# A planned attention and expert kernel: fixing the order of the program on TensorE alone

## Chip, cores and metric

The kernel runs on one core of a Trainium2 chip. The metric is the device time of one execution in microseconds (us). The time before is 265.57 us, the median of three runs (264.77 to 265.9).

The engines are named as in the profile: PE is TensorE (PEld its weight loads), DVE is VectorE, ACT is ScalarE, POOL is GpSimd, and SP only issues DMAs. L143 is line 143 of the kernel.

## What is computed

The input `x` has 2048 tokens of 512 features, in bf16. The result is a sum of three parts:

```
xn  = layernorm(x)
out = x + A(xn) + B(xn)

A: 32 heads of 16 features, the tokens in 4 segments of 512; per segment s
     a_dot = softmax(q k^T / 4 + causal mask) v       within the segment
     a_mem = phi(q) M / (phi(q) z)                     M, z: sums over earlier segments
     o     = g * a_mem + (1 - g) * a_dot
     M    += phi(k)^T v ;  z += sum phi(k)             phi(t) = t + 1 if t > 0, else exp(t)
   A = o @ wo

B: r = xn @ w_r ; the one token with the largest r gets
     (silu(x_sel @ w_gate) * (x_sel @ w_up)) @ w_down * sigmoid(r), added to its row of xn
```

## The kernel before

**Tiles and stages.** Tokens lie in 16 blocks of 128 (`NB`). The attention is walked in 160 steps (`NT`, loop at L735), 40 for each segment. Five steps make a unit of four heads. Each step does three things: `score` (L446) lets PE multiply keys and queries into one of two PSUM tiles `st`; `exp` (L456) lets ACT take the exponential of 128 x 1024 values into `pt` and POOL put zeros above the diagonal (L465); and `pv` (L468) lets PE multiply `pt` with the values into `acc`. In the loop, step t does the exponential of t, the scores of t + 2 and the values product of t - 2 (`LAG = 2`). After each unit DVE divides by the sums (`evac`, L482).

**Fillers.** All other work is written as small generator functions, and at the end of each step `fill` (L646) puts pieces of them between the steps. Each has an earliest step, a due step and a cost in ns of PE's time; `fill` emits so much of them, the most urgent first, that all are done by their due steps. A "pause" in such a function lets some steps pass, so that what it has asked of another engine may be done before PE goes on. The fillers that matter here:

- `g_ln` (L253) does the layer norm of one group of four token blocks. `ln_stats` (L140) lets DVE run BATCH_NORM_STATS2 (L143) and BATCH_NORM_AGGREGATE (L144) on each of the four blocks of `x_all`, `ln_rstd` (L146) takes a logarithm and an exponential on ACT and computes `cvec` (L149) on DVE, `ln_xn` (L153) normalises the four blocks on POOL into the four buffers `xn` (L155), and `ln_T` (L157) transposes each on PE into PSUM, from where DVE copies it to `xnT` (L162). The first group is done in the same way ahead of the loop, with its `xn` on DVE.
- `g_projq`, `g_projk` and `g_projv` (L212, L232, L246) are the projections: PE multiplies into one of two PSUM tiles with the tag `misc`, and DVE moves the result to `raw_q`, `KT` or `Vaug`. SP scatters `raw_q` into `QZ` with eight DMAs.
- `phi_steps` (L191) computes phi with an exponential on ACT (`ex`), a minimum on POOL (`am`) and an addition and a maximum on DVE.
- `g_memT` (L379) transposes phi(k) on PE, and DVE copies it out (`pk`, L385). `g_mem` computes `a_mem` (`nm_ps`, `om`).
- `g_fin` transposes `Oseg`, multiplies with `wo`, adds the row of B and stores 128 tokens. `make_rb` (L490) computes what is added (`rb`, two buffers) on POOL.

**Loads.** SP issues the first four blocks of `x_all` and the weights `wq`, `wk` and `wv` first. ACT issues the other twelve blocks (L701, three DMAs of 512 KB) and `wo` (L702, 512 KB). They stand in the program behind the first group's projections. POOL issues three of the six loads of B's weights (`mw`, L125).

**What sets the order.** Each engine has its own list of instructions and works it in order; an instruction that waits holds up all behind it. A planner makes these lists at compile time. It knows which instruction needs which tile, counts time by its own table of costs, and puts instructions into an engine's list. Between L666 and L766 the program holds it to a rule: for each engine in a given set, the instructions, its DMA issues included, come in the order in which the program emits them. The order between engines, the engines that are not in the set, and the place of instructions from outside of this region stay the planner's. In the kernel before, the set holds PE, ACT, DVE and POOL, so only SP is left. The constants (L81 to L110) and SP's first loads are emitted ahead of the region. The branch for large logits (`slow_path`) comes behind it and isn't taken.

Of the kernel before, what the change touches and what calls it, by code (L numbers as in the profile page):

```python
# [14 lines left out]
ENG = mybir.EngineType  # L15
# [3 lines left out]
def build_kernel(ctx, tc, A_x, A_wq, A_wk, A_wv, A_wo, A_beta, B_x, B_w_r, B_w_gate, B_w_up, B_w_down, out, opts=None):  # L19
# [643 lines left out]
            pass  # L663


    manual = tc.manual_schedule(engines={ENG.PE, ENG.Activation, ENG.DVE, ENG.Pool})  # L666
    manual.__enter__()
    warm_ps = pst.tile([P, 2, L], f32, name="st", tag="st")
    for i in range(14):
# [172 lines left out]
@with_exitstack  # L842
def kernel(
    ctx: ExitStack,
    tc: tile.TileContext,
    A_x: bass.AP,
    A_wq: bass.AP,
    A_wk: bass.AP,
    A_wv: bass.AP,
    A_wo: bass.AP,  # L850
    A_beta: bass.AP,
    B_x: bass.AP,
    B_w_r: bass.AP,
    B_w_gate: bass.AP,
    B_w_up: bass.AP,
    B_w_down: bass.AP,
    out: bass.AP,
):
    build_kernel(ctx, tc, A_x, A_wq, A_wk, A_wv, A_wo, A_beta, B_x, B_w_r, B_w_gate, B_w_up, B_w_down, out)
# [34 lines left out]
```

## Time and profile before

| what | value |
|---|---|
| median of three runs | 265.57 us |
| the profiled execution's own time | 264.61 us |
| its span, from the first to the last instruction | 262.9 us |
| mean granted clock of PE | 0.948 |
| busy PE, ACT, DVE, POOL | 212.2, 177.0, 159.1, 155.0 us |

The span begins with the first instruction of the program and ends with the last; 1.7 us of the profiled execution lie around it. Busy time counts running instructions and not waits or DMA issues. In the lines of the profile, a bracket holds the idle time of the engine just before an instruction and what ended it. In the tables by window, each row has the stretch, its length, the busy us (and count) of PE, PEld, DVE, ACT and POOL, then PE's granted clock, the busy share of the DMA engines and GB/s. In a group's row, `x12 | 9.9, 836` is twelve instructions, 9.9 us together and 836 ns in the mean; behind the next bar is the idle time before them. In a row of the waits, `3.6, 6, 1.5` is us in total, times, and the longest.

### The profile page before, as it was taken

What the parts mean: (1) busy time and instruction counts of PE and PEld (TensorE: products, weight loads), DVE (VectorE), ACT (ScalarE), POOL (GpSimd) and SP (SyncE); (2) the same over time, 40 slices, a digit from 0 to 9 for tenths busy, and PEclk for the clock granted to TensorE, in tenths of its full rate; (3) what the DMA queues carried; (4) which work ended last, traced back from release to release, by engine and by line L of the source; (5) the groups of instructions that cost most, each with busy time, mean ns of one, the idle gap of its engine ahead of it and who ended that gap; (6) DMA issues with size and microseconds to landing.
All of it is one profiled execution on the core that took longest, in us unless ns stands there. A gap on an engine that the chain in (4) does not pass through costs nothing.

```text
span 262.9 us, 6843 instructions
## 1 busy us (share of the span) xinstructions
PE 212.2 (81%) x2677; PEld 138.5 (53%) x2717; DVE 159.1 (61%) x393; ACT 177.0 (67%) x202; POOL 155.0 (59%) x252
## 2 busy tenths in 40 slices
PE   8469977999786967789879888999888888988770
PEld 2224644656453734457555766665766455665530
DVE  6836395248764986355677686755647556565341
ACT  2124986989965968469577876969678587867600
POOL 9501459546629545749768846655568247967530
PEclk9767996899997999999999999999999799999997
DMA  6966510000000000000000004180001010101102
GB/s 187 304 248 185 158 27 16 10 14 13 14 10 10 13 10 6 7 5 18 13 11 10 15 2 143 24 287 17 16 24 29 14 42 21 61 25 40 44 6 87
DMA packets 14186, 14.38 MB, mean 55 GB/s; under 512 B 3184, under 2 KB 13616, under 8 KB 14144
## 3 DMA queue, kind: packets, MB, share of 16 engines
q1 hardware_dynamic: 11456, 9.00, 11.6%
q0 software_dynamic: 576, 2.75, 2.8%
q10 hardware_dynamic: 2112, 2.10, 2.6%
q8 instruction: 23, 0.38, 0.6%
q14 instruction: 19, 0.16, 0.2%
HBM read 9.71 MB, written 2.10 MB: 45 GB/s over the span
## 4 chain that ended last, share of the span: by engine, by line
PE 54%; DVE 26%; ACT 7%; POOL 7%; issue 4%; DMA 1%; DVEq 0%; ACTq 0%
PE st L453 19%; PE proj_ps L206 9%; PE acc L478 7%; ACT pt L458 7%; PE proj_ps L249 5%; POOL xn L155 4%; DVE bnst L143 4%; PE fin L514 4%; DVE om L420 2%; DVE KT L239 2%; DVE Oseg L487 2%; DVE ob L497 2%; DVE xn L155 1%; DVE raw_q L218 1%; POOL pt L465 1%
## 5 line engine op out<-in xcount | busy, mean ns | idle before, releaser
L458 ACT ACTIVATE pt<-st 128x1024 bf16<-128x1024 f32 x160 | 159.5, 1025 | 49.6 <-PE st L453 40.7
L465 POOL TENSOR_SCALAR_AFFINE_SELECT pt<-pt 128x512 bf16<-128x512 bf16 (+1 forms) x160 | 89.5, 567 | 74.0 <-ACT pt L458 72.3
L453 PE MATMUL st<-QZ,KT 128*128 128x256 bf16 (+3 forms) x502 | 96.5, 304 | 7.3 <-ACT pt L458 3.6
L478 PEld LDWEIGHTS <-pt 128*128 128x128 bf16 x1280 | 55.7, 97 | 32.5 <-POOL pt L465 8.3
L478 PE MATMUL acc<-Vaug,pt 128*128 128x17 bf16 x1280 | 56.3, 171 | 6.3 <-POOL pt L465 5.8
L453 PEld LDWEIGHTS <-KT 128*128 128x128 bf16 x512 | 42.4, 98 | 32.8 <-issue 12.4
L206 PE MATMUL proj_ps<-xnT,wk 128*128 128x512 bf16 x60 | 20.3, 408 | 2.4 <-DVE xnT L162 0.9
L485 DVE RECIPROCAL rr<-acc 128x16 f32<-128x16 f32 x32 | 8.2, 255 | 22.7 <-PE acc L478 22.5
L249 PE MATMUL proj_ps<-wv,xnT 128*128 128x512 bf16 x56 | 17.8, 409 | 2.0 <-DVE Vaug L251 0.6
L218 DVE CAST raw_q<-proj_ps 128x512 bf16<-128x512 f32 x15 | 10.4, 690 | 14.6 <-PE proj_ps L206 8.5
L427 POOL TENSOR_TENSOR Oseg<-Oseg,om 128x512 bf16<-128x512 bf16 x11 | 12.7, 1155 | 10.5 <-DVE cvec L149 4.0
L206 PE MATMUL proj_ps<-xnT,wq 128*128 128x512 bf16 x53 | 17.0, 397 | 2.1 <-DVE Vaug L251 1.2
L497 DVE SCALAR_TENSOR_TENSOR ob<-x_all,s,fin 128x512 bf16<-128x512 bf16 x14 | 10.3, 745 | 13.0 <-PE fin L514 10.6
L198 POOL TENSOR_SCALAR am<-ex 128x512 bf16<-128x512 bf16 x24 | 14.8, 617 | 4.5 <-DVE pkT L202 4.2
L251 DVE TENSOR_TENSOR Vaug<-proj_ps,omg_bc 128x512 bf16<-128x512 f32 x16 | 11.0, 690 | 10.0 <-PE proj_ps L249 8.2
L239 DVE CAST KT<-proj_ps 128x512 bf16<-128x512 f32 x15 | 10.3, 684 | 11.3 <-PE proj_ps L206 9.7
L487 DVE TENSOR_TENSOR Oseg<-acc,rr 128x256 bf16<-128x256 f32 x32 | 13.6, 425 | 1.1
L492 POOL TENSOR_SCALAR rb<-ybc,onehot,cvec 128x512 bf16<-128x512 bf16 x16 | 12.6, 793 | 2.2 <-DVE ybc L374 2.2
L155 POOL TENSOR_SCALAR xn<-x_all,rstd,cvec 128x512 bf16<-128x512 bf16 x12 | 9.9, 836 | 5.1 <-DVE cvec L149 5.1
L514 PE MATMUL fin<-wo,oT 128*128 128x512 bf16 x42 | 12.1, 378 | 0.3
L143 DVE BATCH_NORM_STATS2 bnst<-x_all 128x6 f32<-128x512 bf16 x16 | 10.7, 668 | 0.2 <-DMA x_all<-in_A_x_dram 0.2
L160 PE MATMUL pT<-ident,xn 128*128 128x128 bf16 x64 | 7.2, 254 | 3.8 <-DVE xn L155 3.8
(159 smaller groups left out, 250.4 us busy)
## 6 DMA issues: line engine op xcount, KB each, us to landing
out_dram<-ob SPq DMA_DIRECT2D x16, 128.0 KB, 1.7
QZ<-raw_q SPq DMA_DIRECT2D x124, 16.0 KB, 1.8
mw<-in_B_w_gate_dram POOLq DMA_DIRECT2D x2, 896.0 KB, 8.9
mw<-in_B_w_down_dram SPq DMA_DIRECT2D x2, 896.0 KB, 7.0
x_all<-in_A_x_dram ACTq DMA_DIRECT2D x3, 512.0 KB, 5.3
mw<-in_B_w_up_dram POOLq DMA_DIRECT2D x1, 896.0 KB, 11.2
mw<-in_B_w_up_dram SPq DMA_DIRECT2D x1, 896.0 KB, 5.0
x_all<-in_A_x_dram SPq DMA_DIRECT2D x4, 128.0 KB, 2.3
```

The source lines that it names most:

```text
L143: nc.vector.bn_stats(out=st[:], in_=x_all[:, b, :])
L155: eng.tensor_scalar(out=xn[b][:], in0=x_all[:, b, :], scalar1=rstd[:, b:b + 1], scalar2=cvec[:, b:b + 1], op0=ALU.mult, op1=ALU.add)
L206: nc.tensor.matmul(ps[:], lhsT=w[:, cb, j * P:(j + 1) * P], rhs=xnT[:, cb, s * L:(s + 1) * L], start=(cb == 0), stop=(cb == NCB - 1))
L239: nc.vector.tensor_copy(out=kt[:], in_=ps[:])
L249: nc.tensor.matmul(ps[:], lhsT=xnT[:, cb, b * P:(b + 1) * P], rhs=wv[:, cb, :], start=(cb == 0), stop=(cb == NCB - 1))
L453: nc.tensor.matmul(st[:, i, off:off + n], lhsT=lh, rhs=self.qz[:, h, q0:q0 + n], start=True, stop=True)
L458: nc.scalar.activation(out=pt[:], in_=self.st.pop(k)[:], func=ACT.Exp, scale=SCALE)
L465: nc.gpsimd.affine_select(out=mv, in_=mv, pattern=pat, compare_op=ALU.is_ge, fill=0.0, base=0, channel_multiplier=-1)
L478: nc.tensor.matmul(self.acc[:, q0 // P + c, i, e, :], lhsT=pt[:, i, off + c * P:off + (c + 1) * P], rhs=Vaug[:, 4 * self.s + kb, h, :], st ...
L487: nc.vector.tensor_tensor(out=ov, in0=av[:, :, :, 0:DH], in1=rr[:, :, :, None].to_broadcast([P, 4, 4, DH]), op=ALU.mult)
L497: nc.vector.scalar_tensor_tensor(out=ob[:], in0=x_all[:, b, :], scalar=s1[:, b:b + 1], in1=fin, op0=ALU.mult, op1=ALU.add)
L514: nc.tensor.matmul(fin[:], lhsT=oT[:, cb, :], rhs=wo[:, cb, :], start=False, stop=(cb == NCB - 1))
```

## The change

ACT, DVE and POOL leave the set. Only PE keeps the order of the program; the lists of the other three are made by the planner, across the whole region and the constants ahead of it. No instruction is added, removed or given another shape, and the program still emits everything in the same order.

```diff
-    manual = tc.manual_schedule(engines={ENG.PE, ENG.Activation, ENG.DVE, ENG.Pool})
+    manual = tc.manual_schedule(engines={ENG.PE})
     manual.__enter__()
     warm_ps = pst.tile([P, 2, L], f32, name="st", tag="st")
```

## The prediction

> **What bounds the kernel now.** I began with the busy shares and the chain of waits of the profile's page, and then split the body of the run, between the head and the tail, into three stretches with the table of busy times by window.
>
> ```profile
> span 262.9 us, 6843 instructions
> PE 212.2 (81%) x2677; PEld 138.5 (53%) x2717; DVE 159.1 (61%) x393; ACT 177.0 (67%) x202; POOL 155.0 (59%) x252
> ...
> PE 54%; DVE 26%; ACT 7%; POOL 7%; issue 4%; DMA 1%; DVEq 0%; ACTq 0%
> ```
>
> ```profile
> 20.00:70.00 50.00, 44.82 (x485) 27.67 (x491) 28.73 (x64) 40.77 (x49) 27.46 (x48) 0.90 0.20 56
> 70.00:110.00 40.00, 28.44 (x353) 18.86 (x358) 27.39 (x77) 27.46 (x35) 24.45 (x40) 0.96 0.04 11
> 110.00:250.00 140.00, 121.76 (x1770) 84.56 (x1795) 86.39 (x219) 104.21 (x112) 91.54 (x143) 0.99 0.13 40
> ```
>
> TensorE is the busiest engine and works its list strictly in order. DVE is busy 61% of the time, yet it is a quarter of the chain that ended last. So the cost is not DVE's amount of work but work that stands in a bad place of its queue. TensorE idles 5.2 us of 50 in the first stretch, 11.6 of 40 in the second and 18.2 of 140 in the third. The second stretch is the sick one. The timelines say why (start, length, engine, line, what it writes; in brackets the idle time before it and what ended it):
>
> ```profile
> 69.35 0.68 DVE L143 BATCH_NORM_STATS2 bnst<-x_all 128x6 f32<-128x512 bf16 x1
> ...
> 71.76 0.66 DVE L143 BATCH_NORM_STATS2 bnst<-x_all 128x6 f32<-128x512 bf16 x1
> ...
> 73.00 0.71 PE L384 MATMUL pkT_ps<-ident,pkT 128*128 128x128 bf16 x8 [2.50 <-DVE pk L385]
> ...
> 77.58 3.26 POOL L155 TENSOR_SCALAR xn<-x_all,rstd,cvec 128x512 bf16<-128x512 bf16 x4 [4.75 <-DVE cvec L149]
> ...
> 80.80 1.37 POOL L465 TENSOR_SCALAR_AFFINE_SELECT pt<-pt 128x256 bf16<-128x256 bf16 x3
> ```
>
> Four layer-norm statistics of the next 512 tokens run on DVE in one block, from 69.35 to 72.4 us; behind them stands the copy that frees a PSUM buffer, and TensorE waits 2.50 us for it. Then the four normalisations run on POOL in one block of 3.26 us; behind them stand the causal masks, and TensorE waits again. The same two blocks come back for each of the three later token groups:
>
> ```profile
> 39.27 0.60 PE L453 MATMUL st<-QZ,KT 128*128 128x128 bf16 x4 [1.47 <-ACT pt L458]
> ```
>
> ```profile
> 98.73 0.38 PE L418 MATMUL nm_ps<-Mbf,pqT 128*128 128x128 bf16 x4 [1.47 <-DVE KT L239]
> ```
>
> ```profile
> 43.75 0.38 PE L478 MATMUL acc<-Vaug,pt 128*128 128x17 bf16 x8 [1.13 <-POOL pt L465]
> ```
>
> ```profile
> 81.25 0.36 PE L478 MATMUL acc<-Vaug,pt 128*128 128x17 bf16 x8 [2.04 <-POOL pt L465]
> ```
>
> ```profile
> 106.40 0.36 PE L478 MATMUL acc<-Vaug,pt 128*128 128x17 bf16 x8 [2.14 <-POOL pt L465]
> ```
>
> **What the change does, part by part.** It removes no instruction. It takes away the order of the program on ACT, DVE and POOL, so what counts is what the planner puts in its place. The trace shows the planner at work where no order is fixed, in the constants ahead of the region:
>
> ```profile
> 0.81 0.20 POOL L81 MEMSET ident<- 128x128 bf16 x1 [0.29 <-POOLq L878]
> ...
> 0.95 0.10 POOL L84 MEMSET bdsel<- 128x8 f32 x1
> ...
> 1.24 0.29 POOL L82 TENSOR_SCALAR_AFFINE_SELECT ident<-ident 128x128 bf16<-128x128 bf16 x1
> ```
>
> Line 82 stands before line 84 in the program but runs after it, because it has to wait for line 81. So the planner gives an engine the earliest instruction of the program that is ready by the planner's own clock, and pulls later ones forward over one that is not. I take it that it does so everywhere.
>
> (1) Statistics on DVE. Their only input is `x_all`. Its late blocks are loaded by ACT (the page's row of 40 slices shows ACT's busy tenths, 6.6 us each):
>
> ```profile
> ACT  2124986989965968469577876969678587867600
> ```
>
> ```profile
> 21.02 1.58 ACTq L701 DMA_DIRECT2D x_all<-in_A_x_dram  x3
> 22.64 0.53 ACTq L702 DMA_DIRECT2D wo<-in_A_wo_dram  x1
> 23.22 1.94 ACT L458 ACTIVATE pt<-st 128x1024 bf16<-128x1024 f32 x2 [1.98 <-issue]
> ```
>
> These four issues wait for nothing and ACT is 80 to 90% idle in the first three slices, so they should move to about 2 us. With the data there early, the twelve statistics no longer stand as blocks; they go singly into DVE's idle time, mostly before 30 us. The stalls behind them were 1.47 + 2.50 + 1.47 = 5.44 us.
>
> (2) Normalisations on POOL. They follow as soon as one of the four `xn` buffers is free, one at a time, between masks. The stalls behind them were 1.13 + 2.04 + 2.14 = 5.31 us.
>
> Not all 10.75 us come back. In the first stretch ACT is busy 40.77 of 50 us, so of its 2.60 us I count 1.6. The second stretch would, at the third's share of busy TensorE (121.76/140 = 0.87), take 28.44/0.87 = 32.7 us instead of 40: 7.3 us of its 8.15. Together **-8.9**.
>
> (3) The clock. In the two stretches after the first and the second POOL block the granted clock was down:
>
> ```profile
> 38.95:45.78 6.83, 4.61 (x50) 2.79 (x50) 4.19 (x10) 4.81 (x7) 6.51 (x10) 0.65 0.07 18
> 80.00:83.33 3.33, 2.08 (x22) 1.05 (x23) 0.68 (x2) 1.27 (x3) 3.33 (x8) 0.80 0.04 10
> ```
>
> At full clock the 4.61 and 2.08 us of TensorE's work would take between half and all of that: a gain of 0 to 3.3, of which I take **-1.5**. The Trainium skill (TensorE: Matmul & The Clock Gate, What's actually happening) has the clock fall to half only after an idle window of about 3.4 us. By it, taking away idle pieces of 2.5 us and less would bring nothing here and the forecast below would be 257.5; the trace disagrees, since the mean clock was 0.65 and 0.80 with no longer piece in front, and I go by the trace.
>
> (4) The tail. TensorE waits for the first of four POOL operations that need nothing late:
>
> ```profile
> 248.82 3.04 POOL L492 TENSOR_SCALAR rb<-ybc,onehot,cvec 128x512 bf16<-128x512 bf16 x4
> ...
> 249.64 0.38 PE L533 MATMUL fin<-rb,ident 128*128 128x512 bf16 x1 [1.08 <-POOL rb L492]
> ```
>
> They can come earlier as far as the two `rb` buffers allow: **-0.7**, between -1.1 and 0.
>
> (5) The other waits of TensorE after 110 us, of the 18.2 us idle there. They are 0.4 to 1.2 us each, mostly a PSUM eviction on DVE that stood behind another DVE instruction. Some go, others come: **-2**, between -5 and +6.
>
> (6) The head pays for what moves into it.
>
> ```profile
> 6.95 3.88 DVE L155 TENSOR_SCALAR xn<-x_all,rstd,cvec 128x512 bf16<-128x512 bf16 x2
> 8.07 2.30 POOL L706 MEMSET Vaug<- 128x128 bf16 x4
> 11.56 0.73 DVE L155 TENSOR_SCALAR xn<-x_all,rstd,cvec 128x512 bf16<-128x512 bf16 x2
> 13.73 1.87 PE L206 MATMUL proj_ps<-xnT,wk 128*128 128x512 bf16 x4 [0.67 <-ACT xnT L164]
> ```
>
> ```profile
> L143 DVE BATCH_NORM_STATS2 bnst<-x_all 128x6 f32<-128x512 bf16 x16 | 10.7, 668 | 0.2 <-DMA x_all<-in_A_x_dram 0.2
> ...
> L144 DVE BATCH_NORM_AGGREGATE MV<-bnst 128x2 f32<-128x6 f32 x16 | 2.9, 182 | 0.6
> ```
>
> DVE hands over to TensorE some five times between 11 and 20 us (two copies of `xnT`, `KT`, `QZ`, `raw_q`), and a statistic that has just begun holds each up for 0 to 0.85 us (668 + 182 ns): 0 to 4.3 us, with 2.1 at half. The loads: 2.0 MB more in front of the weights.
>
> ```profile
> GB/s 187 304 248 185 158 27 16 10 14 13 14 10 10 13 10 6 7 5 18 13 11 10 15 2 143 24 287 17 16 24 29 14 42 21 61 25 40 44 6 87
> ...
> wk<-in_A_wk_dram SPq DMA_DIRECT2D x1, 512.0 KB, 5.5
> ```
>
> ```profile
> 3.15 0.51 SPq L73 DMA_DIRECT2D wk<-in_A_wk_dram  x1
> ```
>
> `wk` lands at 3.15 + 5.5 = 8.7 us and is wanted at 13.73. If all 2.0 MB went in front at the 304 GB/s of the busiest slice, it would land 6.6 us later, 1.5 us late; shared, it is hardly late. On the other side DVE no longer stands behind ACT's first `rstd`, at most -0.6. I take **+1.5**, between -0.6 and +5.8.
>
> (7) Fillers. Whatever is pulled forward can stand in front of something urgent that comes a moment later on the chip. ACT's 24 `ex` and POOL's 12 `xn` are the long ones:
>
> ```profile
> L155 POOL TENSOR_SCALAR xn<-x_all,rstd,cvec 128x512 bf16<-128x512 bf16 x12 | 9.9, 836 | 5.1 <-DVE cvec L149 5.1
> ...
> L196 ACT ACTIVATE ex<-raw_q 128x512 bf16<-128x512 bf16 x12 | 7.5, 622 | 0.0
> L196 ACT ACTIVATE ex<-KT 128x512 bf16<-128x512 bf16 x12 | 7.5, 630 | 0.0
> ```
>
> All of them on the path would be 24.9 us, none 0. Masks and exponentials run two steps ahead of their use, so I take near the low end, **+2**.
>
> Sum: -8.9 - 1.5 - 0.7 - 2 + 1.5 + 2 = **-9.6 us**. The profiled execution took 264.61 us (span 262.9, 1.7 around it); that gives 255.0. The median of the three timed runs, 265.57, is 1.0 above it, so the forecast for a median is **256 us**.
>
> **The rivals.**
>
> *More comes back (246 us).* If (5) gives its 5 us, the clock its 3.3, all 10.75 us of (1) and (2) come back and the fillers cost nothing, it is 265.6 - 10.75 - 3.3 - 0.7 - 5 + 0.6 = 246. For it speaks that ACT, DVE and POOL are idle for a third or more; against it that many waits after 110 us are round trips from TensorE to DVE and back, which no order shortens.
>
> *POOL holds up DVE in the head (260.5 us).* Two DVE normalisations took 3.88 us beside POOL's issues and memsets and 0.73 us when POOL was quiet. If POOL's next four `xn` (3.3 us by the row at 77.58) and other early work move next to DVE's first ones, the head loses 4.5 us more. The Trainium skill (SBUF — State Buffer, Who interferes with whom) states such a rule: DVE in its two-port modes and GpSimd share a port pair, and the second to issue is fully blocked. The rows at 6.95 and 11.56 agree.
>
> *The planner hardly reorders (265 us).* TensorE's order stays, and most instructions become ready in that order. Against it: the statistics have nothing to wait for.
>
> *Slower (270 us): fillers in front of urgent work.* One mechanism, in the queues of ACT and POOL: the planner's clock is not the chip's. Where it sees an engine idle that on the chip is just about to be needed, it fixes an `ex` or an `xn` in front of an exponential or a mask, and TensorE waits for up to the filler's length. Without (7) the sum is -11.6, so it decides from 11.6/24.9 = 47% of the fillers' time on the path, and at two thirds (16.6 us) the time is 265.6 + 5 = 270.6. For it: TensorE waits already where one stands behind the other (the POOL blocks). Against it: the slack of two steps, and TensorE now waits for ACT's `pt` only here and there:
>
> ```profile
> PE st L453 <- ACT pt L458: 3.6, 6, 1.5
> ```
>
> **How the numbers follow.** Forecast 0.47 (its own range 250 to 261), POOL in the head 0.09, more 0.14, hardly reordered 0.07, slower 0.23. A change below 0.5%, 1.3 us, can't be told from none here. Faster is 0.47 + 0.09 + 0.14 = 0.70, same 0.07, slower 0.23. The range from 246 to 269 leaves out half of "more" and somewhat under half of "slower".
>
> **What would show it.** (1), (2): in the profile after, no four statistics and no four `xn` in a row, the former mostly before 30 us, and TensorE's waits for `pk`, `pt` and `KT` at those places gone; busy TensorE in the second stretch near 87%. (3): no half clock behind them. (6): ACT's loads issued near 2 us, and the first matmul with `wk`, now at 13.73 us, 1 to 2 us later. (7): waits of TensorE for ACT's `pt` well above 3.6 us would speak for the slower case. The forecast is wrong if the statistics keep their places, or if the head grows by over 6 us.

## The result and the profile after

The changed kernel takes 252.38 us in the median of four runs (251.38 to 253.84); the kernel before, on the same chip, takes 265.17 (264.32 to 265.9). The ratio is 0.9523, with a 95% interval from 0.9458 to 0.9588. The profiled execution took 253.84 us, the highest of the four, against 264.61 before; its span is 252.0 us against 262.9. The executions of one kernel differ by up to 2.4% (250.29 to 256.38 us at the widest below), and every stretch and every line of a profile below is of the one profiled execution.

First the page of the kernel after, its summary, the row of granted clock and the chain of waits:

```profile
span 252.0 us, 6891 instructions
PE 209.9 (83%) x2717; PEld 137.3 (54%) x2717; DVE 152.9 (61%) x393; ACT 176.5 (70%) x202; POOL 154.4 (61%) x252
...
PEclk9655569999999999999999999999979999999996
...
PE 56%; DVE 15%; ACT 13%; DMA 7%; issue 3%; POOL 2%; DVEq 0%; SPq 0%; ACTq 0%
```

DVE's share of the chain fell from 26% to 15%, with the same 393 instructions. DMA rose from 1% to 7%: something now waits for a load. The waits of PE, grouped, say where (engine and tile, what it waited for, then us in total, times, and the longest), first after and then before:

```profile
PE pT L160 <- DVE xn L155: 14.7, 1, 14.7
PE st L453 <- ACT pt L458: 1.9, 5, 0.7
...
PE acc L478 <- POOL pt L465: 0.4, 1, 0.4
```

```profile
PE acc L478 <- POOL pt L465: 5.8, 4, 2.1
PE pT L160 <- DVE xn L155: 3.8, 2, 3.3
```

The waits for masks behind the POOL blocks are nearly gone (5.8 to 0.4 us), and one single wait of 14.7 us in the head has come. To add this up, I cut each trace where the same instruction of PE starts, since PE's order is the same in both: the first matmul with `wk` (end of the head), the first L384 weight load, the first L272 weight load, the last L764 weight load, and the end of the span.

| stretch, us | before | after | difference |
|---|---|---|---|
| head | 13.7 | 23.8 | +10.1 |
| A: the loop's first steps | 55.4 | 53.2 | -2.2 |
| B: has the prediction's second stretch (70 to 110 us) and 12 us more | 52.3 | 40.4 | -11.9 |
| C: the rest of the loop | 133.5 | 126.3 | -7.2 |
| tail | 8.0 | 8.3 | +0.3 |

The tables by window at these cuts show how much of it is idle time of PE (first number busy PE; PE's clock is third from the end), before and after:

```profile
13.70:69.10 55.40, 48.21 (x479) 28.38 (x487) 29.93 (x66) 40.97 (x49) 26.72 (x46) 0.88 0.24 76
69.10:121.40 52.30, 38.97 (x500) 26.14 (x506) 34.54 (x92) 37.44 (x47) 32.34 (x52) 0.97 0.05 11
121.40:254.90 133.50, 116.46 (x1676) 80.31 (x1699) 81.62 (x210) 95.14 (x102) 86.25 (x134) 0.99 0.14 42
```

```profile
23.80:77.00 53.20, 48.47 (x487) 28.00 (x487) 31.53 (x73) 40.64 (x52) 32.11 (x53) 0.89 0.05 13
77.00:117.40 40.40, 37.27 (x508) 25.53 (x506) 28.14 (x74) 36.20 (x42) 28.85 (x48) 1.00 0.06 14
117.40:243.70 126.30, 116.48 (x1700) 80.19 (x1698) 79.87 (x206) 96.03 (x102) 83.73 (x132) 0.99 0.15 44
```

In B, PE's idle time falls from 13.3 us to 3.1, and its busy time by 1.7 us at the higher clock (0.97 to 1.00). In C busy PE is the same (116.46 and 116.48), and the 7.2 us are idle time, 17.0 down to 9.8. About 1 us of that may be no idle time: the trace before has 40 matmuls fewer than weight loads (2677 and 2717), 24 of them in C (x1676 against x1700), and where one is missing its time counts as idle. The trace after is the only one here that has them all. The body gained 21.3 us, and the head gave back 10.1 of them.

A has a price of the head in it. After the long wait PE's granted clock stays at half for long: it is 0.50 from 24 to 32 us and 0.56 from 32 to 36, and full behind that up to 77. So PE's busy time in A is no shorter than before (48.47 us against 48.21), though the low clock behind the first POOL block is gone, and A's gain of 2.2 us is all idle time.

The timeline of the head after (start, length, engine, line, in brackets the idle time and its end) shows how:

```profile
0.84 2.84 ACTq L701 DMA_DIRECT2D x_all<-in_A_x_dram  x3
...
3.18 0.51 SPq L73 DMA_DIRECT2D wk<-in_A_wk_dram  x1
...
5.14 0.34 SPq L74 DMA_DIRECT2D beta_bc<-in_A_beta_dram  x1
...
18.98 0.18 DVE L169 TENSOR_SCALAR bcl<-beta_bc 128x32 f32<-128x32 bf16 x1 [9.03 <-DMA beta_bc<-in_A_beta_dram]
...
20.40 0.72 DVE L155 TENSOR_SCALAR xn<-x_all,rstd,cvec 128x512 bf16<-128x512 bf16 x2
...
20.86 1.04 PE L160 MATMUL pT<-ident,xn 128*128 128x128 bf16 x8 [14.67 <-DVE xn L155]
...
23.82 1.86 PE L206 MATMUL proj_ps<-xnT,wk 128*128 128x512 bf16 x4 [0.67 <-ACT xnT L164]
```

Two things happened. ACT's loads went to 0.84 us, and SP's loads, which now run beside them, became late: from issue to landing, after and before,

```profile
wk<-in_A_wk_dram SPq DMA_DIRECT2D x1, 512.0 KB, 13.5
...
beta_bc<-in_A_beta_dram SPq DMA_DIRECT2D x1, 8.0 KB, 13.8
```

```profile
beta_bc<-in_A_beta_dram SPq DMA_DIRECT2D x1, 8.0 KB, 5.9
```

(`wk` had 5.5 us before.) And the planner put `bcl`, a small operation of the gate's constants that reads `beta_bc`, ahead of the first group's `cvec` and `xn` in DVE's list; the program has it behind them, and before it ran at 20.81 us. On the chip `beta_bc` lands at 5.14 + 13.8 = 18.9 us, so DVE stands still for 9.03 us with the normalisation of the first tokens behind it. ACT's second `rstd` stands in the same way behind `eb`, which reads `bcl` (9.57 us idle before 19.19 us).

### The profile page after: what moved, and what is told of

Same layout as the page of the kernel before. It is cut to its first block, busy times and chain, and to the rows that moved or that the text cites. A ratio compares the mean times of both kernels' runs of the same rounds, so it can differ in the third digit from the quotient of the medians.

```text
span 252.0 us, 6891 instructions
## 1 busy us (share of the span) xinstructions
PE 209.9 (83%) x2717; PEld 137.3 (54%) x2717; DVE 152.9 (61%) x393; ACT 176.5 (70%) x202; POOL 154.4 (61%) x252
## 4 chain that ended last, share of the span: by engine, by line
PE 56%; DVE 15%; ACT 13%; DMA 7%; issue 3%; POOL 2%; DVEq 0%; SPq 0%; ACTq 0%
PE st L453 19%; ACT pt L458 12%; PE proj_ps L206 9%; PE acc L478 7%; PE proj_ps L249 6%; DMA beta_bc<-in_A_beta_dram 5%; PE fin L514 4%; DVE ob L497 2%; DVE raw_q L218 2%; DMA x_all<-in_A_x_dram 2%; POOL pt L465 1%; PE fin L511 1%; PE hgu_ps L345 1%; DVE KT L239 1%; DVE tp L200 1%
## 5 line engine op out<-in xcount | busy, mean ns | idle before, releaser
L249 PE MATMUL proj_ps<-wv,xnT 128*128 128x512 bf16 x64 | 20.1, 420 | 1.3 <-DVE KT L239 0.7
L206 PE MATMUL proj_ps<-xnT,wq 128*128 128x512 bf16 x64 | 19.4, 393 | 0.5 <-DVE xnT L162 0.5
L160 PE MATMUL pT<-ident,xn 128*128 128x128 bf16 x64 | 6.7, 240 | 14.9 <-DVE xn L155 14.7
L251 DVE TENSOR_TENSOR Vaug<-proj_ps,omg_bc 128x512 bf16<-128x512 f32 x16 | 11.1, 691 | 9.2 <-PE proj_ps L249 9.1
L198 POOL TENSOR_SCALAR am<-ex 128x512 bf16<-128x512 bf16 x24 | 14.9, 619 | 1.0 <-ACT ex L196 0.2
L514 PE MATMUL fin<-wo,oT 128*128 128x512 bf16 x48 | 13.6, 377 | 0.0
L160 PEld LDWEIGHTS <-xn 128*128 128x128 bf16 x64 | 4.7, 105 | 16.1 <-DVE xn L155 15.2
## 6 DMA issues: line engine op xcount, KB each, us to landing
mw<-in_B_w_up_dram POOLq DMA_DIRECT2D x1, 896.0 KB, 13.7
```

Source lines behind the costliest of these rows:

```text
L198: nc.gpsimd.tensor_scalar(out=am[:], in0=ex[:], scalar1=1.0, scalar2=0.0, op0=ALU.min, op1=ALU.max)
L206: nc.tensor.matmul(ps[:], lhsT=w[:, cb, j * P:(j + 1) * P], rhs=xnT[:, cb, s * L:(s + 1) * L], start=(cb == 0), stop=(cb == NCB - 1))
L249: nc.tensor.matmul(ps[:], lhsT=xnT[:, cb, b * P:(b + 1) * P], rhs=wv[:, cb, :], start=(cb == 0), stop=(cb == NCB - 1))
L514: nc.tensor.matmul(fin[:], lhsT=oT[:, cb, :], rhs=wo[:, cb, :], start=False, stop=(cb == NCB - 1))
```

## The experiments

In kernels with moved code, line numbers are up to four higher or lower. The stretches are cut as above, and each ratio is to the kernel before on the same chip:

| kernel | head | A | B | C | tail | median, us | ratio to before [95%] |
|---|---|---|---|---|---|---|---|
| PE and ACT ordered | 15.4 | 57.6 | 47.6 | 125.7 | 8.6 | 257.56 | 0.969 [0.963, 0.975] |
| all but DVE ordered | 13.8 | 57.3 | 49.0 | 130.0 | 8.2 | 259.4 | 0.976 [0.967, 0.984] |
| all but POOL ordered | 14.9 | 53.9 | 49.5 | 130.5 | 8.7 | 261.01 | 0.984 [0.976, 0.992] |
| after, `beta_bc` first | 22.5 | 52.4 | 40.4 | 125.2 | 8.5 | 249.84 | 0.932 [0.924, 0.940] |
| before, ACT's loads early | 18.6 | 56.9 | 52.1 | 135.2 | 8.4 | 272.92 | 1.021 [1.010, 1.031] |
| before, layer norms spread | 13.7 | 51.1 | 50.8 | 136.2 | 8.2 | 261.13 | 0.979 [0.970, 0.989] |
| after, SP issues the loads | 13.8 | 54.7 | 40.3 | 125.2 | 8.8 | 245.44 | 0.923 [0.914, 0.931] |
| the same, ACT ordered too | 13.8 | 54.7 | 49.8 | 125.7 | 8.8 | 255.1 | none (250.29 to 256.38) |
| before, layer norms early and spread | 13.5 | 51.4 | 43.4 | 133.5 | 8.0 | 254.06 | 0.948 [0.940, 0.956] |
| ACT ordered, statistics early | 13.8 | 56.1 | 40.7 | 127.2 | 8.0 | 246.94 | 0.928 [0.920, 0.935] |
| after, SP issues `mw` as well | 12.9 | 49.9 | 40.3 | 125.2 | 8.1 | 239.77 | 0.896 [0.893, 0.900] |

**Which engine's freedom matters.** The change frees three engines; the first three runs keep one or two of them in the order of the program.

```diff
-    manual = tc.manual_schedule(engines={ENG.PE})
+    manual = tc.manual_schedule(engines={ENG.PE, ENG.Activation})
```

> Order fixed on PE and ACT; DVE and POOL are left to the planner, and ACT's loads of x_all and wo stay behind the first projections. Theory 1 (the head of the changed kernel is lost through ACT's loads moving to 0.84 us, which makes the weights and beta_bc late; the body is gained on DVE and POOL): the first wk matmul is back near 14 us from 23.82, the body keeps its gain, and the time is 240 to 244 us. Theory 2 (the body's gain needs ACT's free order too, because exponentials and ex change places): the head comes back but part of the body's gain goes, 246 us or more.

Theory 1 missed: 257.56 us. The number of theory 2 came true (246 us or more, the head back, part of the body's gain lost), but not by its cause, exponentials and `ex` that change places. The head came back to 15.4, and A, 57.6, and B, 47.6, lost. The timeline of this kernel shows both prices:

```profile
34.17 0.66 DVE L143 BATCH_NORM_STATS2 bnst<-x_all 128x6 f32<-128x512 bf16 x1
34.75 0.67 DVE L218 CAST raw_q<-proj_ps 128x512 bf16<-128x512 f32 x1
...
35.48 0.38 PE L206 MATMUL proj_ps<-xnT,wq 128*128 128x512 bf16 x1 [4.36 <-DVE raw_q L218]
...
96.50 0.29 ACT L147 ACTIVATE lnv<-MV,eps_col 128x4 f32<-128x4 f32 x1
...
97.33 3.02 POOL L155 TENSOR_SCALAR xn<-x_all,rstd,cvec 128x512 bf16<-128x512 bf16 x4 [0.25 <-DVE cvec L149]
```

A row of statistics (that at 34.17 is among the last) stands in front of an eviction, and PE waits 4.36 us: ACT's loads are back at their late place, and DVE's list has the statistics early. And `lnv` on ACT keeps its place in the program, so all four `xn` on POOL become ready together at 97.33 and run in one block again, though POOL is free to move them. How this reaches PE is shown below, with the kernel in which ACT alone makes the difference.

With ACT and POOL in the order and DVE free (`{PE, Activation, Pool}`), and with ACT and DVE in it and POOL free (`{PE, Activation, DVE}`):

> Only DVE is left to the planner; PE, ACT and POOL keep the program's order. Theory 1: the stalls behind the statistics (5.4 us) and most DVE waits after 110 us go, the three stalls behind POOL's xn blocks (5.3 us) stay: 252 to 256 us. Theory 2 (POOL's order carries the gain): 260 us or more.

> Only POOL is left to the planner. Theory 1: the xn blocks break up, the statistics blocks on DVE stay, so at most the 5.3 us behind xn come back: 259 to 263 us. Theory 2 (POOL's order carries the gain): 255 us or less.

The first, 259.4 us, lies between the cases; the second is as expected. Each keeps the stall of the engine that it holds to the order (`pt` behind POOL's block in the one, `pk` behind DVE's block in the other):

```profile
102.23 0.36 PE L478 MATMUL acc<-Vaug,pt 128*128 128x17 bf16 x8 [2.11 <-POOL pt L465]
```

```profile
72.57 0.71 PE L384 MATMUL pkT_ps<-ident,pkT 128*128 128x128 bf16 x8 [2.50 <-DVE pk L385]
```

In C they gain 3.5 and 3.0 us, and the run with both free gains 7.8. Of idle time of PE alone it is 2.8 and 2.4 us against 5.1 (the rest of the 7.8 is busy time at a clock of 1.00 instead of 0.99): there the gains of DVE and POOL add up, and ACT's freedom is not needed.

**What the head lost.** The changed kernel with the 8 KB load of `beta_bc` moved to the front of SP's loads:

```diff
+    nc.sync.dma_start(out=beta_bc[:], in_=A_beta.partition_broadcast(P))
...
-    nc.sync.dma_start(out=beta_bc[:], in_=A_beta.partition_broadcast(P))
```

> The changed kernel, with the 8 KB load of beta_bc issued ahead of the first x_all block on SP; ACT's loads still early. Theory 1 (DVE's list in the head is held by bcl, which waits 9.0 us for beta_bc, and behind it only wk, landing at 16.7 us, is late): the first wk matmul starts at about 17 us in place of 23.82, and the time is 245 to 247 us. Theory 3 (contention of the loads alone costs the head its 10 us, bcl only shows it): 251 to 253 us.

Neither case came true; 249.84 us lies between them. The wait for `beta_bc` is gone, but the head is only 1.4 us shorter, because `wk` is late by itself, and lands later than in the changed kernel (16.9 us from issue to landing instead of 13.5):

```profile
7.81 0.69 DVE L143 BATCH_NORM_STATS2 bnst<-x_all 128x6 f32<-128x512 bf16 x1 [5.10 <-DMA x_all<-in_A_x_dram]
...
13.86 0.70 DVE L155 TENSOR_SCALAR xn<-x_all,rstd,cvec 128x512 bf16<-128x512 bf16 x2
...
22.46 1.89 PE L206 MATMUL proj_ps<-xnT,wk 128*128 128x512 bf16 x4 [5.88 <-DMA wk<-in_A_wk_dram]
```

To have the loads alone, I moved them in the kernel before, with all four engines ordered:

```diff
+    for s in range(1, NSEG):
+        nc.scalar.dma_start(out=x_all[:, 4 * s:4 * s + 4, :], in_=x_d[:, 4 * s:4 * s + 4, :])
+    nc.scalar.dma_start(out=wo[:], in_=A_wo.rearrange("(cb p) n -> p cb n", p=P))
     ln_stats(0, 2)
```

(The same lines are taken out at L700.)

> The kernel before with the order of the program fixed on all four engines, and only ACT's four loads (x_all blocks 4 to 15, wo) emitted ahead of the first layer-norm statistics. Theory 3 (contention of the loads alone costs the head its 10 us): wk is late, the first wk matmul starts at 20 us or later in place of 13.73, and the time is 270 us or more. Theory 1 (DVE's wait for beta_bc in the planner's list costs most of it): the first wk matmul starts near 17 us, and the time is 267 to 270 us.

```profile
18.57 1.89 PE L206 MATMUL proj_ps<-xnT,wk 128*128 128x512 bf16 x4 [5.52 <-DMA wk<-in_A_wk_dram]
```

The first matmul with `wk` starts between the two cases, and the time, 272.92 us, is that of theory 3. The head grows by 4.8 us from the loads alone, and the rest of the kernel gains nothing from having `x_all` early (B 52.1, C 135.2). In the changed kernel, with the wait of `bcl`, it is 5.2 us longer still. The two can't simply be added: without that wait, the late `wk` set the head by itself, at 18.6 us here and at 22.5 in the run before.

Next, the changed kernel with these four loads issued by SP behind its own (and taken away from ACT), so that they don't start before `wk`:

```diff
+    for s in range(1, NSEG):
+        nc.sync.dma_start(out=x_all[:, 4 * s:4 * s + 4, :], in_=x_d[:, 4 * s:4 * s + 4, :])
+    nc.sync.dma_start(out=wo[:], in_=A_wo.rearrange("(cb p) n -> p cb n", p=P))
```

> The changed kernel (order fixed on PE alone) with ACT's four loads issued by SP instead, behind the weights. Theory 1 and 3 agree on the head (the weights come first again): the first wk matmul back at 13 to 15 us and the body as in the changed kernel, 240 to 245 us. If the order that the planner makes does not fit the landing times (statistics in front of casts, as with order fixed on PE and ACT): 247 us or more.

The head is back at 13.8 and the body stays fast: 245.44 us, just above the case. What is left is a place where the planner's order doesn't fit the landing times (its own clock is not in the trace; I read it from the order). In front of DVE's `QZ` stands a statistic that waits for its block:

```profile
18.82 0.69 DVE L146 BATCH_NORM_STATS2 bnst<-x_all 128x6 f32<-128x512 bf16 x1 [2.42 <-DMA x_all<-in_A_x_dram]
...
20.22 0.58 PE L456 MATMUL st<-QZ,KT 128*128 128x512 bf16 x1 [2.84 <-DVE QZ L696]
```

**Where the body's gain comes from.** If the blocks of the layer norm are the cause, spreading them by hand in the kernel before, all engines ordered, should bring it. The first try took the work of each group at about its old time, a block per step (L254 and the rest of `g_ln`'s work ahead of `ln_T` taken out):

```diff
+        for g, r in ((1, 10), (2, 38), (3, 54)):
+            if t in range(r - 6, r - 2):
+                ln_stats(4 * g + t - r + 6, 4 * g + t - r + 7)
+            if t == r - 1:
+                ln_rstd(4 * g, 4 * g + 4)
+            if t in range(r - 1, r + 6, 2):
+                ln_xn(4 * g + (t - r + 1) // 2, nc.gpsimd)
```

> The kernel before, all four engines in the order of the program, TensorE's order untouched; only the statistics and normalisations of the three later token groups are emitted one block in a step instead of four in a row. Theory 4 (these blocks are the body's loss): their stalls of 10.75 us and the half clocks behind them go: 253 to 258 us. Theory 5 (the planner's order of everything else carries the gain): 260 us or more.

It takes 261.13 us, the number of theory 5. It gains 4.3 us in A, but B gains 1.5 and C loses 2.7. Statistics of single steps still land ahead of an eviction (here `xnT`) that PE is waiting for. Three of them, from 84.81, 85.63 and 87.96 us on, stand with their aggregates ahead of it, and three other DVE operations among them; PE waits 3.79 us:

```profile
87.96 0.68 DVE L143 BATCH_NORM_STATS2 bnst<-x_all 128x6 f32<-128x512 bf16 x1
...
88.78 0.39 DVE L162 COPY xnT<-pT 128x512 bf16<-128x512 bf16 x1
...
89.22 1.01 PE L206 MATMUL proj_ps<-xnT,wk 128*128 128x512 bf16 x2 [3.79 <-DVE xnT L162]
```

The second try has SP issue the loads and takes the work of each group earlier and, but for the first group's statistics, two or three steps apart:

```diff
+        for g, ss, r, xs in ((1, (2, 3, 4, 5), 7, (8, 10, 12, 14)), (2, (12, 14, 16, 18), 20, (24, 27, 30, 33)), (3, (22, 25, 28, 31), 34, (43, 46, 49, 52))):
+            if t in ss:
+                ln_stats(4 * g + ss.index(t), 4 * g + ss.index(t) + 1)
+            if t == r:
+                ln_rstd(4 * g, 4 * g + 4)
+            if t in xs:
+                ln_xn(4 * g + xs.index(t), nc.gpsimd)
```

> The kernel before with the order of the program fixed on all four engines and TensorE's order untouched; late x_all blocks loaded by SP behind the weights, and the twelve late statistics and normalisations emitted singly, two to three steps apart and as early as the data and the xn buffers allow. Theory 4 (the blocks behind each other are the second stretch's loss, and the planner's part in it is only to take them out of the way): the stalls at pk, KT and pt of the second stretch go and the time is 254 to 258 us; the third stretch stays as before. Theory 5 (the planner's order of everything else carries the gain): 260 us or more.

```profile
65.00:108.00 43.00, 36.71 (x488) 24.95 (x493) 30.00 (x74) 35.80 (x42) 29.08 (x48) 1.00 0.05 13
108.00:242.00 134.00, 116.92 (x1686) 80.58 (x1706) 81.82 (x210) 95.33 (x102) 86.36 (x134) 0.99 0.14 42
```

(The two windows are rounded to whole microseconds.) It takes 254.06 us, at the lower end of theory 4. B falls from 52.3 to 43.4 with no planner at work on ACT, DVE and POOL, and C stays at 133.5. So the blocks are three quarters of B's gain (8.9 of 11.9): 7.0 us of PE's idle time (13.3 to 6.3) and 1.9 us of its busy time at the higher clock. C's 7 to 8 us are none of theirs; by what is left, they come from the planner's order of other work on DVE and POOL.

**Why ACT must be free, or `rstd` early.** The kernel with SP's loads and with ACT put back into the order:

> As the kernel with SP's loads, but the order of the program is fixed on PE and ACT. Theory 6 (ACT's two short instructions for rstd, kept at their places, keep POOL's xn in blocks, and that is why fixing ACT lost part of the body's gain): 3 to 6 us more than with SP's loads, and four xn in a row near 100 us. Theory 7 (it was only the late loads): the same as with SP's loads.

Its four times lie 4.9 to 10.9 us above the kernel with SP's loads, where theory 6 has 3 to 6, and in the profile the difference lies in B: 49.8 us against 40.3, with all other stretches within 0.5 us. Of the 9.5 us, 4.9 are idle time of PE and 4.5 busy time at a lower clock (0.90 against 1.00). ACT's `lnv` at its place in the program again starts four `xn` in a row:

```profile
93.25 0.29 ACT L150 ACTIVATE lnv<-MV,eps_col 128x4 f32<-128x4 f32 x1
...
94.08 3.02 POOL L158 TENSOR_SCALAR xn<-x_all,rstd,cvec 128x512 bf16<-128x512 bf16 x4 [0.25 <-DVE cvec L152]
...
98.09 3.48 DVE L205 TENSOR_TENSOR pkT<-tp,am 128x512 bf16<-128x512 bf16 x1 [1.87 <-POOL am L201]
...
101.50 0.68 DVE L254 TENSOR_TENSOR Vaug<-proj_ps,omg_bc 128x512 bf16<-128x512 f32 x1
...
102.23 0.59 PE L163 MATMUL pT<-ident,xn 128*128 128x128 bf16 x4 [3.04 <-DVE Vaug L254]
```

The way from the block to PE leads over DVE. POOL is busy with the four `xn` until 97.10 us, so `am` comes late (DVE idles 1.87 us for it), and one addition and four masks then run back to back on POOL. DVE's addition takes 3.48 us beside them (more on this in the last section), `Vaug` stands behind it, and PE waits 3.04 us. The run with PE and ACT ordered has the same rows, with a wait of 3.0 us, and the two with ACT free have none like it.

The test of this reading moves the statistics and `rstd` of the three groups, ACT still ordered; in ACT's list only `lnv` and `rstd` change their places, and DVE is left to the planner in both kernels (the two calls in `g_ln` are taken out):

```diff
+        if t in (7, 14, 21):
+            g = t // 7
+            ln_stats(4 * g, 4 * g + 4)
+            ln_rstd(4 * g, 4 * g + 4)
```

> As the kernel with SP's loads and the order fixed on PE and ACT, but the statistics and rstd of the three later token groups are emitted at steps 7, 14 and 21, so that ACT's two short instructions stand earlier in its fixed list; DVE and POOL are left to the planner as there. Theory 6 (ACT's place of rstd is what keeps the four xn together near 100 us): the stall of 3.04 us there goes, and the time comes to within 2 us of the kernel with SP's loads, 243 to 247 us. Theory 8 (ACT's fixed order costs by the exponentials and ex instead): 250 us or more.

B is 40.7 and the time 246.94, within 2 us of the kernel with SP's loads as theory 6 has it: what ACT's freedom is worth in B is the place of three `lnv` and three `rstd`. Its span is 3.0 us longer than with ACT free: C by 2.0, and A by 1.4, where a statistic now waits 4.17 us for its block, and PE 4.9 us for the `QZ` behind it:

```profile
20.58 0.69 DVE L146 BATCH_NORM_STATS2 bnst<-x_all 128x6 f32<-128x512 bf16 x1 [4.17 <-DMA x_all<-in_A_x_dram]
```

**A version that beats both.** In the kernel with SP's loads, POOL's three issues of `mw` go to SP too, so that all early loads leave from one queue:

```diff
-    gate_consts()
...
-        load_mw(kind, hf, nc.gpsimd)
+        load_mw(kind, hf, nc.sync)
+    gate_consts()
```

> The kernel with SP's loads and order fixed on PE alone, and also POOL's three 896 KB loads of mw issued by SP behind wo. If the loads of mw hold up the late x_all blocks (a statistic in front of QZ waits 2.42 us for one) and POOL's issues hold up DVE's first xn: first wk matmul 1 to 3 us earlier than 13.8, no wait for x_all in front of QZ, and 238 to 242 us. If the scatter of raw_q into QZ falls behind mw in SP's queue: 245 us or more.

```profile
span 236.4 us, 6848 instructions
PE 203.9 (86%) x2677; PEld 135.6 (57%) x2717; DVE 154.1 (65%) x393; ACT 176.6 (75%) x202; POOL 152.2 (64%) x249
```

239.77 us, as expected, a ratio to before of 0.8963 (0.893 to 0.8997). Against SP's loads alone, A falls by 4.8 us and the head by 0.9; B and C are the same. In the head the first two `xn` on DVE take 3.30 us instead of 5.00 without POOL's issues beside them. In A, PE's wait for `QZ` falls from 2.8 to 0.8 us, because the late blocks of `x_all` land 5.6 to 7.3 us earlier (the first at 13.23 us instead of 18.80) and no statistic stands waiting; and PE's busy time falls from 47.04 to 45.21 us, at a granted clock of 0.96 instead of 0.89.

## Why the prediction was right and wrong

The sign and the range held, and the time is 3.6 us under the forecast. That closeness is partly luck: the head cost 8.6 us more than the sum said, and the body gained 10.2 more (21.3 against 8.9 + 1.5 + 0.7 + 2 - 2 = 11.1).

- *The planner's rule* (it takes the earliest instruction that is ready by its own clock): right, as far as the order shows it. ACT's loads went to 0.84 us, against "near 2 us", and fourteen of the sixteen statistics had started by 30.1 us, the last starts at 37.98. (The row of ACT's tenths, 2, 1, 2 in the first slices, means 70 to 90% idle, not 80 to 90; nothing hangs on it.)
- *(1), (2) the blocks, -8.9*: the mechanism is right, and for the blocks alone the size too. Of four `xn` in a row only the first group's is left, at 32.94; the others run singly. A gained 2.2 (forecast 1.6). In B the early, spread layer norms take away 7.0 us of idle time by themselves (forecast 7.3), and PE is then busy 37.01 of 43.30 us, 85%, near the third stretch's 87% that I took. The changed kernel takes away 10.2 and comes to 37.27 of 40.40, 92%. The 3.2 us between them are no blocks: among them are PE's waits of 1.2 us for `Vaug`, 0.8 for `om` and 0.6 for `Mrun`, which the early, spread layer norms keep and the changed kernel hasn't. The prediction had such waits in (5), but only after 110 us.
- *What (1), (2) left out*: that ACT's `lnv` and `rstd` decide when POOL's `xn` become ready. I costed DVE and POOL as if ACT's part didn't matter, and the two runs with ACT ordered and `rstd` late have a B that is 7.2 and 9.5 us longer than with ACT free, 5.6 and 4.9 us of it idle time of PE.
- *(3) the clock, -1.5*: the lower clock behind the POOL blocks is gone; the row of granted clock is full from the seventh slice to the last but one, but for a single slice. The 1.7 us of B fit the term in size, and only B gives them: in A the half clock that the longer head leaves behind, until 36 us, takes back what the first block gave. That B's clock rose from 0.97 to 1.00 when idle pieces of 2.5 us and less went bears against the Trainium skill (TensorE: Matmul & The Clock Gate, What's actually happening), by whose idle window of about 3.4 us, read as idle throughout, nothing was to be gained here. The mean over the span fell (0.948 to 0.929) by the half clock in the longer head and behind it.
- *(4) the tail's `rb`, -0.7*: the 1.1 us wait is gone from PE's waits.
- *(5), (7) other waits -2, fillers +2*: together 0 forecast, and C gained 7.2, of which (4) has about 1. The prediction kept the third stretch's busy share as a limit; it was itself in part the work of the order on DVE and POOL, 2.8 and 2.4 us of idle time. No cost of the fillers shows on ACT's or POOL's queue: PE's waits for ACT's `pt` fell from 3.6 to 1.9 us, and those for POOL's from 5.8 to 0.4.
- *(6) the head, +1.5 with an upper end of 5.8*: the step that failed, at +10.1. It priced the `wk` load by bandwidth, at worst 6.6 us later, and counted on sharing to make that less. `wk` took 8.0 us longer to land (13.5 against 5.5); in the run that has only ACT's loads early (15.4 to landing) this cost 4.8. And it counted DVE's hand-overs without asking which instruction of DVE would now wait for a late load with everything behind it: `bcl` for `beta_bc`. It is the same greed that I had described, applied to a load that lands later on the chip than the planner's order allows for. The prediction's own mark, a head that grows by over 6 us, was passed; that the time was close all the same is due to the body.
- *The rivals*: "More comes back" describes the body, not the whole. "POOL holds up DVE in the head" didn't happen there: two `xn` took 0.72 us at 20.40. But the first two took 5.00 us in the kernel with SP's loads, so the mechanism is there: PE waits 4.21 us for them, though the head is no longer than before. "Slower by fillers" has the right mechanism in the wrong queue: work in front of urgent work was seen on DVE (4.36 us with ACT ordered, 2.84 us with SP's loads), where statistics stand in front of evictions or wait for a block; behind statistics the longest single wait of PE was 4.9 us, with ACT ordered and the statistics early. "Hardly reorders" was wrong.

What stays open is which of the planner's moves in C, and in B beside the blocks, give which part of the 7 and the 3 us: I have the stretches and the waits, and no run that takes the moves apart.

## What to carry to other kernels

Freeing an engine from the program's order frees its DMA issues as well: list every load that it issues and every instruction that reads a late load, and ask what would stand behind it in the queue before you price the compute. Long optional work on the side engines (here the layer norm of the next tokens) costs by where it stands, and a chain over several engines can be moved only if every engine of it may move: here three logarithms with their exponentials on ACT, left in their old places, held back about 5 us of TensorE's time, and up to as much again through the clock. Loads that are wanted in a certain order were best on one queue in this order here: the ratio to the kernel before went from 0.952 over 0.923 to 0.896.

## What was unexpected of the hardware

A small load was as late as the large one ahead of it in its queue: with 2.0 MB more issued early by ACT, the 8 KB of `beta_bc` took 13.8 us from issue to landing instead of 5.9, and the 512 KB of `wk` 13.5 instead of 5.5. A small broadcast load at the head of a queue isn't free either. With it first, the four 128 KB blocks of `x_all` took 7.4 us to land (the median of the four) instead of 2.3 before and 4.5 after:

```profile
x_all<-in_A_x_dram SPq DMA_DIRECT2D x4, 128.0 KB, 7.4
...
wk<-in_A_wk_dram SPq DMA_DIRECT2D x1, 512.0 KB, 16.9
...
beta_bc<-in_A_beta_dram SPq DMA_DIRECT2D x1, 8.0 KB, 4.7
```

One DVE addition was stretched eightfold beside POOL. In the run with PE and ACT ordered it began just behind POOL's `Oseg`, and ended with POOL's masks (104.8 and 104.5 us); before, the same line took 0.43 us:

```profile
101.27 1.15 POOL L427 TENSOR_TENSOR Oseg<-Oseg,om 128x512 bf16<-128x512 bf16 x1
101.34 3.48 DVE L202 TENSOR_TENSOR pkT<-tp,am 128x512 bf16<-128x512 bf16 x1 [1.87 <-POOL am L198]
...
102.37 2.17 POOL L465 TENSOR_SCALAR_AFFINE_SELECT pt<-pt 128x512 bf16<-128x512 bf16 x4
```

```profile
91.73 0.43 DVE L202 TENSOR_TENSOR pkT<-tp,am 128x512 bf16<-128x512 bf16 x1
```

The Trainium skill (SBUF — State Buffer, Who interferes with whom) says that a DVE instruction with two SBUF inputs contends with a GpSimd instruction that reads SBUF. The trace agrees, and adds that the wait lasted over five POOL instructions in a row. Where POOL's next instruction began just after DVE's addition, the addition took its usual time: 0.43 and 0.41 us in the same run, at 62.84 and 65.28 us, with POOL's masks 0.15 and 0.06 us behind. An ordered queue can thus be late by another engine's work that it doesn't wait for.
